# New engine orders for a fused linear-attention and squared-ReLU feed-forward kernel

## The chip, the cores and the metric

The kernel runs on one core of a Trainium2 chip. The metric is the device time of one execution in microseconds; the lower it is, the better. Three runs of the kernel before gave 171.85, 172.10 and 172.58 us, with a median of 172.1. One further execution was profiled; all rows below come from it.

## The reference

The first stage is a gated linear attention, a recurrence over 768 positions with a 48 x 48 state for each of 4 x 8 heads. The second is a feed-forward layer with a squared ReLU.

```python
# q, k, v, alpha: (4, 8, 768, 48), float32
for t in range(S):
    state = alpha[:, :, t, :, None] * state + np.einsum('bhd,bhe->bhde', k[:, :, t], v[:, :, t])
    y[:, :, t] = np.einsum('bhd,bhde->bhe', q[:, :, t], state)
x = y.transpose(0, 2, 1, 3).reshape(3072, 384)
h = x @ w_in                 # (384, 2048)
r = np.maximum(h, 0.0)
out = (r * r) @ w_out        # (2048, 384)
```

## The kernel before

**Units.** The 3072 tokens are cut into 12 units of 256 (four batches, three stretches of each). A unit's number stands in every name of the order: `p0_4` is the score step of unit 4.

**Attention of a unit g.** Four loads bring alpha, k, q and v (`lda`, `ldk`, `ldq`, `ldv`, lines 521 to 540) into one of four raw buffers. `pr` multiplies pairs of alpha, `ln` takes the logarithm, a matmul with a triangular matrix (`m1`, later `m1i` and `m1s`) makes running sums in PSUM, and `ei`, `ea`, `ec`, `es` take exponentials on ScalarE (`lm` and `lb` make the second set from unit 4 on; `bk` and `aq` multiply by alpha). `ekm` and `eqm` multiply k and q by them on VectorE. The results are transposed: for units 0 to 2 on TensorE (`tr`, with the copies `et` out of PSUM), from unit 3 on by two DMA transposes (`tr0_g`, `tr1_g`, line 745) that SyncE issues. `p0` makes the scores of all heads in two PSUM tensors, `mk0` and `mk1` (line 934) apply the causal mask on VectorE, `vc` casts v to bf16, `kv` makes the state's products (from unit 3 on inside the step `y` of the unit before), `sa`, `sc` and `sd` update the state, and `y` (lines 801 to 870) makes the attention's output in PSUM. `xe` copies it out, `xt` transposes it, on TensorE with the copy `xv` for units 0 to 6 and by a DMA transpose for units 7 to 11 (the tuple `DMA_X`, line 369).

**Feed-forward of a unit.** `s1_g_u` for u = 0 to 7 are the first layer's groups, six matmuls of 256 columns each; `re` is the ReLU of one group and `sq` the square of one or two (lines 1035 and 1045 to 1049). The second layer is plain for units 0, 1, 2 and 11 (`s2_g_j_s`: token half j, quarter s of the hidden width, four matmuls of 384 columns; `oe` copies the result out). For units 3 to 10 it is one level of Strassen's scheme (lines 1061 to 1142): seven products `m1` to `m7` in two halves each (`s2_g_m10` is the first half of m1; four matmuls of 192 columns), sums of the weights made once (`ws`), sums of the activations (`ga`, `gb`, `gc`, a half each, lines 1077 to 1080), and copies and additions `ca` to `cg` that collect the products in the output tile. `out` is the store of a unit.

**The order.** The dictionary `ORDERS` (lines 12 to 77) writes out for each of the five engines the list of names that it executes, one after the other; it also says which engine does a step that could be done by several (`RING`, line 79). Steps without a name have a number: `#0` to `#23` are the constants' fills. `Program.place` finds which earlier steps of other engines each step has to wait for, and `Program.emit` writes for each engine its list with these waits. An engine waits at the head of its list, so what stands behind a waiting step waits too. `lda` to `ldv`, `win`, `wout`, `tr`, `xt` and `out` are DMAs: in the list of SyncE (`sp`) or GpSimd (`pool`) stands their issue. `fill512` and `fill256` are matmuls on zeros in the list of TensorE (`pe`); nothing reads what they write. Some loads have a gate besides (the table `AFTER`): `lda2`, `ldk2`, `ldq2` and `ldv2` go out after `win1` has landed, `wout0` after `win2`, `wout1` after `ldk2`, the loads of unit 3 after `wout0`, `ldq1` and `win1` after `ldk0`.

**PSUM.** Eight banks of 2 KB: two `psX` and two `psZ` for the attention (`psZ` holds also the state products and, from unit 5 on, the running sums), `psWH` with one bank for the second layer (`W`) and two for the first (`H`), and `psO` for the second layer. `s2_2_1_0` writes `psO` after `oe2_0` has read it. Output tiles are two, used in turn: `oe2_0` writes the tile that `out0_1` stores.

Of the kernel before, what the change touches and what calls it, by code (L numbers as in the profile page):

```python
# [18 lines left out]
        ec7 re4_5 sq4_3 re4_6 es7 sq4_6 re4_7 re5_0 sq4_5 re5_1 lm8 re5_2 re5_3 ln8 xe6 ei8 ea8 re5_5 re5_4 es8 cc4
        re5_7 sq5_1 re5_6 lm9 sq5_3 sq5_6 re6_1 re6_0 xe7 ln9 re6_2 ei9 ea9 re6_4 re6_5 ca5 sq6_5 re6_6 es9 cc5 re6_7  # L20
        sq6_3 re7_0 lm10 re7_1 vc10 re7_2 ln10 xe8 ei10 ea10 re7_4 re7_5 sq7_3 re7_7 sq7_1 re7_6 re8_1 sq7_5 cc6 es10
        xe9 re8_2 sq7_6 ln11 sq7_7 lm11 ei11 ea11 es11 re8_5 ca7 re8_6 sq8_5 re8_7 sq8_1 re9_0 vc11 sq8_3 re9_1 re9_2
        xe10 re9_3 re9_5 re9_4 sq9_1 re9_7 re10_1 cc8 re10_3 re10_4 re10_5 sq10_1 re10_6 cc9 sq10_5 re11_1 sq10_7
# [11 lines left out]
        gc6_1 sa10 cd6 ce6 re8_4 ga7_1 re8_3 cg6 cf6 lb11 eqm1_11 gb7_1 eqm0_11 mk1_10 cb7 ekm11 cc7 mk0_10 sq8_7 cd7
        ce7 ga8_0 gb8_0 ga8_1 cg7 sa11 gb8_1 gc8_0 sq9_3 gc8_1 ca8 cf7 re9_6 mk1_11 sq9_7 re10_0 cb8 mk0_11 ga9_0
        re10_2 cd8 ce8 xe11 gb9_0 gb9_1 cf8 cg8 ca9 re10_7 sq10_6 cb9 re11_0 cd9 ce9 ga10_1 cg9 re11_2 gb10_1 gb10_0
        cf9 gc10_1 cc10 cb10 re11_4 cd10 ce10 sq11_5 cg10 re11_6 cf10 oe11_0 oe11_11
# [1222 lines left out]
```

## Time and profile before

| | us |
|---|---|
| median of three runs | 172.1 |
| lowest and highest | 171.85, 172.58 |
| profiled execution, its own time | 172.4 |
| span of the profiled execution | 170.7 |
| HBM read and written | 25.17 MB, 4.72 MB |

The span runs from the first to the last instruction of the profile; the execution's own time has 1.7 us more around it. A row of a timeline reads: start, duration, engine, line, operation, output tile from input tiles, form and count, and in brackets how long the engine stood idle just before and which event ended that wait. A row of a group has the busy time and the mean in ns of one instruction behind the bar. PE is TensorE (PEld its weight loads), DVE VectorE, ACT ScalarE, POOL GpSimd and SPq the queue of SyncE. Matmuls are pipelined: the duration of one includes its drain, and the pace is read from start to start. The releaser of a wait is inferred from semaphores: where the engine named had long been done it was another, often a DMA.

### The profile page before, as it was taken

Reading aid. Unit: us, or ns where it says so; the run is one execution under the profiler, and the core shown is the slowest. Engines: PE = TensorE matmul, PEld = TensorE weight load, DVE = VectorE, ACT = ScalarE, POOL = GpSimd, SP = SyncE. Lnnn points to the kernel's source line nnn. Section 1 sums busy time; section 2 is a strip of 40 time slices with the busy share of each in tenths; the row PEclk is TensorE's granted clock in tenths of the full one; section 3 lists DMA queues with packets and bytes.
Section 4 is the critical chain, followed back from the end, with each engine's and each line's share of the span. In section 5 each row is a group of like instructions: output and inputs, shape, how many; then the busy total and the mean of one; then the engine's idle time right before and its main releaser. Section 6 shows DMA issues by size and latency. Waiting matters only on the chain.

```text
span 170.7 us, 5620 instructions
## 1 busy us (share of the span) xinstructions
PE 162.1 (95%) x2428; PEld 140.2 (82%) x2428; DVE 137.0 (80%) x243; ACT 120.6 (71%) x213; POOL 89.1 (52%) x85
## 2 busy tenths in 40 slices
PE   6899999799999969999999999989999999999994
...
DMA  5999999998999999999999789999864920400222
GB/s 135 338 272 252 289 280 197 245 336 213 160 252 158 284 296 140 318 206 289 199 202 313 150 145 267 189 235 282 116 149 79 183 96 4 119 23 0 92 96 94
DMA packets 68233, 32.81 MB, mean 192 GB/s; under 512 B 64144, under 2 KB 65168, under 8 KB 68208
## 3 DMA queue, kind: packets, MB, share of 16 engines
...
HBM read 25.17 MB, written 4.72 MB: 175 GB/s over the span
## 4 chain that ended last, share of the span: by engine, by line
PE 60%; DMA 19%; DVE 10%; POOL 5%; SPq 2%; issue 1%; ACT 1%; DVEq 0%
PE psWH L1027 22%; PE psO L1093 11%; PE psWH L1093 9%; DMA raw<-in_k_dram 7%; DMA wout<-in_moe_w_out_dram 5%; PE psO L1165 5%; DMA win<-in_moe_w_in_dram 4%; DMA raw<-in_v_dram 3%; DVE pm L934 3%; DVE qks L734 3%; PE psX L826 2%; PE psZ L794 2%; PE psX L815 2%; PE psX L995 2%; PE psX L923 2%
## 5 line engine op out<-in xcount | busy, mean ns | idle before, releaser
L1027 PE MATMUL psWH<-xt,win 128*128 128x256 bf16 x552 | 72.1, 273 | 0.1
L1027 PEld LDWEIGHTS psWH<-xt,win 128*128 128x128 bf16 x552 | 59.8, 129 | 1.5 <-DVE xt L981 0.3
L1035 ACT ACTIVATE rr<-psWH 128x512 bf16<-128x512 f32 x73 | 42.4, 595 | 20.7 <-PE psWH L1027 19.9
L1049 ACT ACTIVATE gt<-rr 128x1024 bf16<-128x1024 bf16 (+1 forms) x37 | 33.9, 928 | 1.2 <-DVE rr L1037 1.1
L1048 POOL TENSOR_TENSOR gt<-rr 128x512 bf16<-128x512 bf16 (+1 forms) x11 | 16.3, 1479 | 19.6 <-ACT rr L1035 19.6
L1165 PE MATMUL psO<-wout,gt 128*128 128x384 bf16 x96 | 18.4, 326 | 1.2 <-DMA wout<-in_moe_w_out_dram 1.2
L934 DVE TENSOR_TENSOR pm<-psZ,caus 128x1024 bf16<-128x1024 f32 x12 | 14.6, 1219 | 2.4 <-PE psZ L923 2.4
L934 DVE TENSOR_TENSOR pm<-psX,caus 128x1024 bf16<-128x1024 f32 x12 | 14.6, 1216 | 1.4 <-PE psZ L923 1.1
L1080 POOL TENSOR_TENSOR sh<-gt 128x512 bf16<-128x512 bf16 x10 | 13.1, 1314 | 5.0 <-DVE gt L1079 3.7
L1093 PE MATMUL psWH<-sw,gt 128*128 128x192 bf16 x128 | 15.5, 246 | 0.0
L1037 DVE TENSOR_SCALAR rr<-psWH 128x512 bf16<-128x512 f32 x19 | 13.0, 686 | 3.0 <-PE psWH L1027 3.0
L1093 PE MATMUL psO<-wout,gt 128*128 128x192 bf16 x128 | 14.0, 246 | 0.0
L1165 PEld LDWEIGHTS psO<-wout,gt 128*128 128x128 bf16 x96 | 8.7, 97 | 6.2 <-DMA wout<-in_moe_w_out_dram 1.5
L734 DVE TENSOR_TENSOR qks<-raw,ek 128x768 bf16<-128x768 f32 x11 | 11.6, 1052 | 2.3 <-DMA raw<-in_k_dram 1.6
L1079 POOL TENSOR_TENSOR gt<-sg,gt 128x512 bf16<-128x512 bf16 x7 | 9.8, 1404 | 6.2 <-DVE sg L1077 6.1
L683 POOL TENSOR_TENSOR ek<-ek,raw 128x384 f32<-128x384 f32 x9 | 9.0, 1005 | 6.6 <-ACT ek L676 6.6
L1077 POOL TENSOR_TENSOR sg<-gt 128x1024 bf16<-128x1024 bf16 x3 | 6.4, 2132 | 9.7 <-PE psO L1093 8.3
L1093 PEld LDWEIGHTS psWH<-sw,gt 128*128 128x128 bf16 x128 | 10.9, 98 | 0.5
L729 DVE TENSOR_TENSOR qks<-raw,eq 128x384 bf16<-128x384 f32 x18 | 10.8, 612 | 0.3 <-ACT eq L702 0.2
L1077 DVE TENSOR_TENSOR sg<-gt 128x1024 bf16<-128x1024 bf16 x13 | 10.7, 824 | 0.3 <-PE psO L1093 0.2
L1093 PEld LDWEIGHTS psO<-wout,gt 128*128 128x128 bf16 x128 | 10.6, 98 | 0.4
L1124 DVE TENSOR_TENSOR osb<-psWH,osb 128x192 f32<-128x192 f32 x24 | 8.4, 352 | 2.4 <-PE psWH L1093 2.4
...
## 6 DMA issues: line engine op xcount, KB each, us to landing
raw<-in_q_dram SPq DMA_DIRECT2D x11, 384.0 KB, 5.8
out_dram<-osb SPq DMA_DIRECT2D x11, 384.0 KB, 4.2
raw<-in_alpha_dram SPq DMA_DIRECT2D x10, 384.0 KB, 4.5
raw<-in_k_dram SPq DMA_DIRECT2D x9, 384.0 KB, 5.2
raw<-in_v_dram SPq DMA_DIRECT2D x9, 384.0 KB, 4.9
...
raw<-in_k_dram POOLq DMA_DIRECT2D x3, 384.0 KB, 6.3
raw<-in_v_dram POOLq DMA_DIRECT2D x3, 384.0 KB, 7.6
```

The costliest lines, as they stand in the source:

```text
L729: add("dve", lambda e, j=j, dst=dst: e.tensor_tensor(dst, RAW[r][:, 2, :, j, :].rearrange("p (n x) d -> p n x d", x=2), EQ[la][:, j].rearr ...
L734: add("dve", lambda e, a=a, E=E: e.tensor_tensor(QKS[qs][:, a, :, :, 0:D], RAW[r][:, 1 + a].rearrange("p h j d -> p j h d"), E[la][:].rear ...
L934: add("dve", lambda e, hf=hf, psT=psT: e.tensor_tensor(PM[pm][:, hf].rearrange("p r n j t -> p (r n) (j t)"), psT[:, :, :].rearrange("p r ...
L1027: ins = pe.matmul(psF[:, i * T:(i + 1) * T], WIN[:, kk, hidden(fj)], mov, start=(kk == 0), stop=(kk == KT - 1))
L1035: add("act", lambda e, psF=psF, rr=rr: e.activation(rr, psF, AF.Relu), act_ns(512), pu + 600, reads=[keyF], writes=[("rr", rb, half)], nam ...
L1037: alts={"dve": (lambda e, psF=psF, rr=rr: e.tensor_scalar(rr, psF, 0.0, None, ALU.max), dve_ns(512))})
L1048: alts={"pool": (lambda e, dst=dst, sq=sq: e.tensor_tensor(dst, sq, sq, ALU.mult), 200 + k * 840), "act": (lambda e, dst=dst, sq=sq: e.act ...
L1049: "act": (lambda e, dst=dst, sq=sq: e.activation(dst, sq, AF.Square), act_ns(k * 512))})
L1077: ga = lambda e, us=us: e.tensor_tensor(SG[:, us], view(us, 128, [[0, 2], [1, 128]]), view(us, 0, [[384, 2], [1, 128]]), ALU.subtract)
L1080: gc = lambda e, us=us: e.tensor_tensor(SH[:, us], G4[:, us, 1, 0], G4[:, us, 0, 1], ALU.add)
L1093: ins = pe.matmul(psS, left(u), right(u), start=(first and u == 0), stop=(u == nu - 1), skip_group_check=True)
L1165: ins = pe.matmul(psS, GT[gt][:, fj, j, :], WOUT[:, fj, :], start=(fj == 0), stop=(fj == FT - 1))
```

## The change

Only the text of `ORDERS` is changed. Its diff is cut to what is spoken of later; the other lines of the five lists are likewise rewritten.

```diff
     "act": """
-        table ln0_0 ln1_0 ei0_0 ea0_0 ei1_0 ec0_0 et00_0 ea1_0 ec1_0 #23 et01_0 et11_0 ln1 ei1 ea1 xe0 ec1 et0_1 re0_1
-        vc1 re0_0 sq0_1 re0_3 xe1 re0_4 ln2 re0_6 ei2 re0_7 es2 vc2 re0_5 ea2 re1_1 re1_3 sq0_6 et0_2 ec2 sq0_7 sq1_3
...
+        table #23 ln0_0 ln1_0 ei0_0 ea0_0 ei1_0 ea1_0 et00_0 ec1_0 ec0_0 vc0 et11_0 ln1 ei1 ea1 xe0 xv0 ec1 vc1 re0_0
+        re0_1 re0_2 re0_3 sq0_1 re0_4 ln2 re0_7 ei2 sq0_3 re0_5 es2 ea2 sq0_5 re1_3 re1_4 re1_5 ec2 re1_6 et1_2 re1_7
...
     "dve": """
-        et1_2 re1_4 ws0_0 ws2_0 re1_6 mk1_2 pr3 sq1_7 ws0_1 sa2 mk0_2 ekm3 sc2 eqm1_3 aq3 eqm0_3 pr4 oe1_0 xv2 sa3 sc3
-        lb4 ekm4 eqm1_4 eqm0_4 mk0_3 mk1_3 re2_5 oe1_1 xe3 sa4 xv3 sq2_7 sc4 lb5 eqm1_5 ekm5 mk1_4 mk0_4 eqm0_5 ws1_0
...
-        mk1_8 ga6_0 cd5 sq6_7 sa9 ce5 re7_3 gc5_0 lb10 cf5 ga6_1 ekm10 cg5 mk1_9 ca6 mk0_9 cb6 re8_0 eqm1_10 eqm0_10
...
+        eqm2 et0_2 #4 ws0_0 ws2_0 ws3_0 mk1_2 pr3 ws0_1 sa2 sc2 mk0_2 ekm3 eqm1_3 aq3 pr4 eqm0_3 oe1_0 sa3 xv2 ws2_1
+        sc3 lb4 eqm1_4 eqm0_4 ekm4 mk1_3 mk0_3 re2_5 ws1_0 xe3 sa4 sc4 sq2_7 xv3 bk5 eqm1_5 lb5 ekm5 mk1_4 mk0_4
+        eqm0_5 oe2_0 sa5 sc5 ga3_0 ws1_1 xv4 re3_7 lb6 eqm1_6 eqm0_6 ekm6 mk1_5 mk0_5 ca3 ga3_1 re4_2 sa6 sc6 gc3_0
...
+        eqm1_9 eqm0_9 mk0_8 mk1_8 cd5 re7_1 re7_2 ce5 sa9 re7_3 ga6_1 gb6_0 re7_5 cf5 cg5 lb10 ekm10 mk1_9 mk0_9
...
+        ekm11 mk1_10 gc7_0 sq8_7 cd7 sd7 ga8_0 ce7 ga8_1 sa11 cg7 gb8_0 cf7 sq9_3 mk0_11 cb8 mk1_11 cc8 cd8 re10_1
+        ga9_1 ga9_0 ce8 cf8 re10_5 cg8 re10_6 gc9_0 ca9 cb9 cc9 cd9 ce9 re10_7 cg9 re11_2 ca10 ga10_1 cf9 re11_3 cb10
...
     "pe": """
-        fill256_8 tr01_0 fill256_9 p0_0 tr11_0 kv0 fill256_10 p1_0 fill256_11 fill256_12 m11 y0 fill512_13 fill512_14
-        fill512_15 fill256_16 tr0_1 xt0 tr1_1 fill256_17 s1_0_1 p0_1 s1_0_0 s1_0_2 kv1 s1_0_3 y1 s1_0_4 s1_0_6 xt1
-        s1_0_7 m1i2 m1s2 s1_1_2 s1_1_0 s1_1_1 s1_0_5 s1_1_3 s1_1_5 tr0_2 s1_1_4 tr1_2 s1_1_6 s2_0_0_0 p0_2 s2_0_0_1
-        s1_1_7 s2_0_0_2 s2_0_0_3 s2_0_1_0 kv2 m1i3 s2_0_1_1 s2_1_0_0 s2_0_1_2 s2_1_0_1 m1s3 s2_1_0_2 y2 s2_1_0_3
-        s2_0_1_3 xt2 m1i4 s2_1_1_0 s1_2_0 s1_2_1 s2_1_1_1 s1_2_2 s1_2_3 p0_3 s1_2_4 s1_2_5 s2_1_1_2 s2_1_1_3 y3 s1_2_6
-        s1_2_7 xt3 m1i5 s2_2_0_0 s1_3_0 s1_3_1 p0_4 s2_2_0_1 s1_3_2 s1_3_3 s2_2_0_2 s2_2_0_3 y4 s1_3_5 s1_3_4 m1i6
-        s2_2_1_0 s1_3_7 s2_2_1_1 xt4 s2_2_1_2 s2_2_1_3 s1_3_6 p0_5 s1_4_1 s1_4_0 s2_3_m10 s2_3_m11 s2_3_m60 s1_4_2
...
-        s2_5_m40 s1_7_3 s2_5_m41 m1i10 s1_7_4 s1_7_5 s2_5_m30 s2_5_m31 s1_7_6 s1_7_7 p0_9 s2_6_m60 s2_6_m10 s2_6_m11
...
+        fill512_8 fill256_9 fill256_10 tr01_0 p0_0 tr11_0 kv0 fill256_11 p1_0 fill256_12 fill256_13 m11 fill256_14 y0
+        fill512_15 fill512_16 fill512_17 tr0_1 xt0 tr1_1 fill512_18 fill512_19 fill512_20 fill256_21 p0_1 s1_0_0
+        s1_0_2 s1_0_1 kv1 s1_0_3 y1 s1_0_4 s1_0_6 s1_0_7 xt1 m1i2 m1s2 s1_0_5 s1_1_1 s1_1_2 s1_1_0 tr0_2 s1_1_4 s1_1_3
+        s1_1_5 s1_1_6 s1_1_7 tr1_2 s2_0_0_0 s2_0_0_1 p0_2 s2_0_1_0 s2_0_0_2 s2_0_0_3 kv2 m1i3 s2_0_1_1 s2_1_0_0
+        s2_1_0_1 s2_1_0_2 m1s3 s2_0_1_2 y2 s2_1_0_3 s2_0_1_3 xt2 m1i4 s2_1_1_0 s1_2_0 s1_2_1 s2_1_1_1 s1_2_2 s1_2_3
+        p0_3 s2_1_1_2 s1_2_5 s1_2_4 s2_1_1_3 y3 s2_2_0_0 s1_2_7 s1_2_6 xt3 m1i5 s2_2_0_1 s2_2_0_2 s1_3_0 s1_3_1 p0_4
+        s1_3_2 s1_3_3 s2_2_0_3 s1_3_4 y4 s2_2_1_0 s1_3_5 m1i6 xt4 s2_2_1_1 s1_3_7 s2_2_1_2 s2_2_1_3 s1_3_6 s1_4_1 p0_5
...
+        s2_5_m71 s1_7_1 s2_5_m50 s1_7_2 y8 s2_5_m51 s1_7_3 s2_5_m40 s1_7_4 s2_5_m41 s2_5_m30 m1i10 s1_7_5 s2_5_m31
+        s1_7_6 s1_7_7 s2_6_m10 s2_6_m11 p0_9 s2_6_m20 s2_6_m60 s1_8_0 s1_8_1 s2_6_m21 s1_8_2 y9 s2_6_m61 s2_6_m50
...
+        s2_8_m11 s2_8_m61 s1_10_1 s1_10_0 s2_8_m20 s2_8_m21 s2_8_m70 y11 s2_8_m71 s1_10_2 s2_8_m50 s2_8_m51 s1_10_3
+        s2_8_m40 s1_10_4 s2_8_m41 s1_10_5 s2_8_m30 s2_8_m31 s1_10_6 s2_9_m10 s2_9_m60 s2_9_m61 s2_9_m11 s1_11_0
...
     "pool": """
-        #22 #15 #14 #21 #20 lda1 ldk1 win0 vc0 win1 ldv1 win2 lda2 ldq2 ldk2 ldv2 wout0 wout1 aq2 sq1_1 ldk3 ldv3
-        ws3_0 bk3 pr6 sd2 bk4 vc4 pr5 ws2_1 sd3 bk5 vc5 sd4 gb3_0 bk6 sq3_6 vc6 gb3_1 gc3_1 sd5 bk7 sq4_7 vc7 pr8
...
-        gb7_0 bk11 gc7_1 sq8_6 sd7 gc7_0 sq9_5 sq9_6 ga9_1 gc9_0 gc9_1 sq10_3 ga10_0 gc10_0 sq11_7
+        #15 #21 #22 #20 #14 lda1 win0 ldk1 ldq1 win1 ldv1 win2 lda2 ldk2 ldq2 ldv2 wout0 sd1 wout1 vc2 aq2 sq0_7 sq1_3
+        ldk3 ldv3 sq1_7 bk3 pr6 sd2 bk4 vc4 sd3 pr5 sq2_5 vc5 sd4 sq3_3 gb3_0 bk6 sq3_6 vc6 pr7 gb3_1 sd5 bk7 sq4_7
...
+        sd6 pr11 gc6_1 gb7_0 gb7_1 vc11 bk11 gc7_1 gb8_1 sq9_7 sq9_5 gc8_1 gc8_0 gb9_0 gb9_1 gc9_1 sq10_6 ga10_0
+        sq10_7 gb10_0 gb10_1 gc10_0 sq11_3 sq11_5 sq11_7
     """,
     "sp": """
-        lda0 ldk0 ldq0 ldv0 ldq1 lda3 ldq3 lda4 lda6 ldq4 ldk4 tr1_3 tr0_3 ldv4 lda5 ldq5 tr1_4 tr0_4 ldk5 ldv5 out0_1
-        ldq6 ldk6 out1_1 tr0_5 tr1_5 ldv6 lda7 ldq7 ldk7 out2_1 tr1_6 tr0_6 ldv7 lda8 ldk8 ldv8 tr1_7 tr0_7 ldq8 lda9
-        ldk9 ldv9 ldq9 out3_1 tr0_8 tr1_8 xt7 lda10 ldv10 ldk10 tr1_9 lda11 tr0_9 xt8 out4_1 ldq10 ldq11 ldk11 out5_1
...
+        lda0 ldk0 ldq0 ldv0 lda3 ldq3 lda4 lda6 ldq4 ldk4 tr0_3 tr1_3 ldv4 lda5 ldk5 ldq5 tr0_4 tr1_4 ldv5 out0_1 ldk6
+        ldq6 out1_1 tr0_5 tr1_5 ldv6 lda7 ldq7 ldk7 tr0_6 tr1_6 ldv7 lda8 ldk8 out2_1 tr0_7 tr1_7 ldq8 ldv8 lda9 ldv9
+        ldk9 ldq9 out3_1 tr0_8 tr1_8 xt7 lda10 ldv10 ldk10 tr0_9 out4_1 tr1_9 xt8 ldq10 lda11 ldv11 out5_1 ldq11
...
```

Counted over the whole text, 160 names stand on another engine than before: 28 go from ScalarE to VectorE and 27 back, 19 from VectorE to GpSimd and 12 back, 9 from ScalarE to GpSimd and 7 back, and one load (`ldq1`) moves from SyncE's list to GpSimd's. TensorE's list has 14 fills of 512 columns and 8 of 256, before 10 and 8. Nothing outside `ORDERS` is touched.

68 lines of the change are left out of this document (32 added, 36 removed).

## The prediction

> **What bounds the kernel now.** I read the page's busy shares and slices first, then the busy time by stage, then TensorE's own timeline for the places where it stands still, and last the chain of waits and the SyncE, VectorE and GpSimd timelines around each of those places.
>
> ```profile
> PE 162.1 (95%) x2428; PEld 140.2 (82%) x2428; DVE 137.0 (80%) x243; ACT 120.6 (71%) x213; POOL 89.1 (52%) x85
> PE   6899999799999969999999999989999999999994
> DMA  5999999998999999999999789999864920400222
> ```
>
> TensorE is the bound, with two dents in the middle (slices 8 and 15, near 32 and 62 us). The DMA engines are full until 85 us, so loads have a floor of their own there. By stage:
>
> ```profile
> 16.00:36.00 20.00, 18.43 (x263) 15.47 (x264) 16.56 (x27) 14.71 (x25) 11.37 (x11) 1.00 1.06 260
> 36.00:62.00 26.00, 24.48 (x384) 18.50 (x384) 21.43 (x35) 19.79 (x39) 10.59 (x11) 1.00 1.02 231
> 62.00:74.00 12.00, 12.00 (x234) 10.46 (x226) 10.73 (x19) 11.30 (x22) 5.08 (x5) 1.00 1.23 254
> ...
> 110.00:122.00 12.00, 11.29 (x189) 10.69 (x188) 9.75 (x18) 9.53 (x17) 6.84 (x6) 1.00 0.99 228
> ```
>
> The first column after the length is TensorE's busy time, and the granted clock is 1.00 throughout. Up to 62 us it misses 1.6 and 1.5 us; from 62 to 74 nothing, and the slices read nine until 110; from there 0.7. So an order can win little but the stalls, and they have names:
>
> ```profile
> 34.36 1.48 PE L1165 MATMUL psO<-wout,gt 128*128 128x384 bf16 x8 [1.23 <-DMA wout<-in_moe_w_out_dram]
> 48.01 0.42 PE L923 MATMUL psX<-kqt 64*64 64x128 bf16 x16 [0.24 <-DVE qks L729]
> 61.63 0.19 PE L815 MATMUL psX<-sbd,kqt 64*128 64x48 bf16 x1 [1.28 <-DVE pm L934]
> 113.06 0.42 PE L923 MATMUL psX<-kqt 64*64 64x128 bf16 x16 [0.71 <-DVE osb L1124]
> ```
>
> In the order's names these are `s2_0_0_2` (second half of w_out), `p0_3`, `y4` and `p0_9`; together 3.46 us.
>
> **The change part by part.** No instruction of the computation changes. 160 names change engine, nearly all names change place, and TensorE gets four more 512-column fills. That units 4 to 6 transpose x on TensorE is in the kernel before already (`DMA_X` starts at 7, and the row below counts six transposes for each of units 0 to 6), so this costs and saves nothing.
>
> ```profile
> L969 PE MATMUL psX<-ident,xbf 128*128 128x128 bf16 x42 | 3.5, 219 | 0.0
> 13.36 0.93 PE L1228 MATMUL psO<-zero 128*128 128x512 bf16 x4
> 15.94 0.68 DVE L764 COPY kqt<-psZ 128x1024 bf16<-128x1024 bf16 x1
> ```
>
> *Fills and opening.* Four fills are about 0.9 us (the row holds three of 512 and one of 256). Four of the new list (three of 512, one of 256) stand between `tr1_1` and `p0_1`, which waits for `et1_1` until 16.6 anyway (the copy's row), so they fill a wait. Then `p0_1` comes before any group of `s1_0`, and TensorE goes into 17 us about 0.4 us behind. Ahead of the wait for w_out, `s2_0_1_0` (four matmuls, 0.65 us in the chain's steps) is now put before `s2_0_0_2`. So TensorE reaches w_out's second half with 0.65 more done, and up to all 1.23 us of that stall can go. But the next stop is `p0_3`:
>
> ```profile
> 38.91 0.96 DVE L734 TENSOR_TENSOR qks<-raw,ek 128x768 bf16<-128x768 f32 x1 [0.25 <-POOL ek L683]
> 39.78 0.55 DVE L896 TENSOR_TENSOR tmp<-psZ,smd 128x384 f32<-128x384 f32 x1
> 41.89 3.35 SPq L745 DMA_TRANSPOSE kqt<-qks  x2
> kqt<-qks SPq DMA_TRANSPOSE x18, 4.7
> ```
>
> `p0_3` reads the transposed keys and queries of unit 3. The two transposes are issued at 41.89, as soon as `eqm0_3` is done, the second about 1.7 us later (43.6); with the median landing of 4.7 us that is 48.3, where `p0_3` in fact starts at 48.01. VectorE's `eqm0_4`, which the wait row names, is nothing that `p0_3` reads, so I take the transposes for the cause. In the new VectorE order `sc2` (0.55) leaves the stretch from `ekm3` to `eqm0_3` and `pr4` enters it, of the same length (0.555 in its group); the start of that stretch hangs on unit 3's alpha, whose load waits for w_out's first half. So this floor stays at 48.0, and I count the opening at **0**. Its bounds: 1.23 us gained if the floor moves up as well, 1.7 lost if unit 3's loads come late (first rival).
>
> `ldq1` moves from SyncE, where it went out at 5.43, to GpSimd's queue behind `lda1`, `win0` and `ldk1`, about 7.1 by my count of three issues from 4.4 on, some 0.9 each (`ldv3`'s row further down). The one q load of that queue took 7.1 to land: so it lands near 14.2, when `eqm1` begins at 14.23. If it is 0.8 late, that is covered by the same floor.
>
> ```profile
> 5.43 0.37 SPq L537 DMA_DIRECT2D raw<-in_q_dram  x1
> 14.23 0.95 DVE L734 TENSOR_TENSOR qks<-raw,eq 128x768 bf16<-128x768 f32 x1
> raw<-in_q_dram POOLq DMA_DIRECT2D x1, 384.0 KB, 7.1
> ```
>
> *The stall at 61.63.* The chain of waits goes from the transposes of unit 4 to unit 5's k, to `ekm5`, to the two mask products of unit 4 behind it on VectorE, to `y4`:
>
> ```profile
> 48.57 4.93 SPq L745 DMA_TRANSPOSE kqt<-qks  x2
> 53.54 1.36 SPq L537 DMA_DIRECT2D raw<-in_k_dram  x1
> 55.60 1.11 SPq L1181 DMA_DIRECT2D out_dram<-osb  x1
> 56.34 0.42 PE L923 MATMUL psX<-kqt 64*64 64x128 bf16 x16
> 58.35 0.96 DVE L734 TENSOR_TENSOR qks<-raw,ek 128x768 bf16<-128x768 f32 x1 [1.60 <-DMA raw<-in_k_dram]
> 59.31 2.28 DVE pm L934 x2
> 62.68 1.53 PE L1027 MATMUL psWH<-xt,win 128*128 128x256 bf16 x12
> 61.89 0.49 ACT L1172 ACTIVATE osb<-psO 128x384 f32<-128x384 f32 x1 [1.99 <-DMA out_dram<-osb]
> ```
>
> `ldk5` now stands ahead of `ldq5` and of both transposes, so k lands before 54 instead of 58.26, and `ekm5` (behind `bk5`, which VectorE now does in 0.56) can run by 57.5. The transposes go out 1.4 us later (one load's issue); `p0_4` has two more groups of `s2_2` before it (1.3 us) as cover. After `p0_4` (near 57.65) two mask products need 2.3, and TensorE has four groups, 2.6 us, to do. The 1.28 us go. Part comes back at once: behind `y4` stands `s2_2_1_0`, which writes the bank that `oe2_0` empties; `oe2_0` (now on VectorE, 0.555) waits for the store `out0_1`, whose issue has the same steps ahead of it as before and so its 55.60, and which landed at 61.89. So `s2_2_1_0` starts about 62.5, when `y4` (some 1.0 long, 61.63 to 62.65) would have ended at 61.9 with `s1_3_4` done. Before, the group behind `y4` began at 62.68, so `y4` ended near 62.65, without `s1_3_4` (0.66, half of that row's two groups from start to start). Gain 62.65 - 62.5 + 0.66 = **0.81** (ends 0 and 1.28).
>
> *The stall at 113.06.* `s2_6_m10` and `m11` (0.33 each, four matmuls) now come before `p0_9` instead of behind it, and `cg5`, which frees their bank, no longer queues behind `ga6_1` and `ekm10`. Whatever `p0_9` waits for, the second transpose of unit 9 by my reading (106.83 plus 4.7 to 6.1), they fill 0.66 of 0.71. Between unit 9's transposes `out4_1` takes the place of `lda11`, 0.58 each:
>
> ```profile
> 106.21 0.58 SPq L537 DMA_DIRECT2D raw<-in_alpha_dram  x1
> 106.83 2.48 SPq L745 DMA_TRANSPOSE kqt<-qks  x1
> 110.68 0.58 SPq L1142 DMA_DIRECT2D out_dram<-osb  x1
> ```
>
> Gain **0.66** (ends 0 and 0.71).
>
> *Moved work.* Priced by the groups' means, the moves give GpSimd 14.4 us more, and take 3.7 from VectorE and 1.5 from ScalarE, so loads become 103, 133 and 119 us under TensorE's 162: none becomes the bound by its sum. By place a move can hurt, above all a half-sum of the second layer, of which GpSimd makes three times the time:
>
> ```profile
> L1079 POOL TENSOR_TENSOR gt<-sg,gt 128x512 bf16<-128x512 bf16 x7 | 9.8, 1404 | 6.2 <-DVE sg L1077 6.1
> L1079 DVE TENSOR_TENSOR gt<-sg,gt 128x512 bf16<-128x512 bf16 x9 | 4.1, 476 | 0.0
> L1077 DVE TENSOR_TENSOR sg<-gt 128x1024 bf16<-128x1024 bf16 x13 | 10.7, 824 | 0.3 <-PE psO L1093 0.2
> 127.62 1.53 DVE L734 TENSOR_TENSOR qks<-raw,ek 128x768 bf16<-128x768 f32 x1
> 128.30 1.87 POOL L1080 TENSOR_TENSOR sh<-gt 128x512 bf16<-128x512 bf16 x1
> ```
>
> New stalls that I can't place: nothing at the low end, at the high end 1.28, the largest that this kernel has; I take 0.2, about its smallest, since every stall that I could trace got ready work put in front of it.
>
> **Sum** against the profiled execution: 172.4 - 0.81 - 0.66 + 0.2 = 171.1 (span 169.4). The runs' median lies 0.3 under that execution, so 170.8.
>
> **The rivals.** *The opening gives it back.* GpSimd now issues `ldk3` and `ldv3` behind `vc2`, `aq2`, `sq0_7` and `sq1_3`; before, behind `aq2` and `sq1_1`, `ldv3` at 31.80. For it: ScalarE now squares `sq0_3` and `sq0_5` ahead of `re1_3`, which `sq1_3` reads. If that makes the loads 2.7 us late, v of unit 3 lands near 41.5 (34.5 and some 7 of the 7.6 that is the median there), its cast on ScalarE ends at 42.3, and `y2`, now at 40.64, is 1.7 late, and the floor with it: 172.1 - 1.47 + 1.7 = 172.3. Against it: my count of ScalarE's new order gives only 0.5 us.
>
> ```profile
> 31.80 0.89 POOL L537 DMA_DIRECT2D raw<-in_v_dram  x1
> raw<-in_v_dram POOLq DMA_DIRECT2D x3, 384.0 KB, 7.6
> 40.64 0.36 PE L855 MATMUL psX<-smd,kqt 128*64 128x96 bf16 x8
> ```
>
> *Slower: the half-sums.* In units 7, 9 and 10 both `gb` halves run one after the other on GpSimd. From `s2_8_m51` to `s2_9_m61` TensorE has 4.6 us of other groups; the path through `ga9_1`, `ga9_0` (0.82 each) and `gb9_0`, `gb9_1` (1.40 each) is 4.44. One collision with VectorE stretched `ekm10` from 0.96 to 1.53 and the sum beside it from 1.16 to 1.87. From the first collision in a unit on, it is late by about 0.5, with two by 1.1; and 1.1 in each of units 9 and 10, with 0.9 for the squares of unit 11 that queue behind them, is 3.1 (unit 7 has 0.9 us of slack by the same count): 172.1 - 1.47 + 3.1 = 173.7. By the Trainium skill ("SBUF — State Buffer", Who interferes with whom) VectorE and GpSimd hold a shared port as an exclusive lock for a whole instruction, so a collision would cost up to a full GpSimd operation, 1.4; with two in each of two units that is near 5 us, about 176. Rows agree that they collide, at 0.6 to 0.7.
>
> *More than forecast.* The loads' floor moves up too (w_out's first half earlier, as `win1` and `win2` no longer queue on GpSimd behind the cast `vc0`) and the 1.23 go as well: 169.6. Against it: full DMA engines.
>
> **Chances.** Forecast 0.40 (its own range 170.1 to 171.6), opening gives back 0.22, half-sums 0.26, more than forecast 0.12. No change means within 0.5%, 0.86 us, about what the runs can tell. Faster: 0.36 of the forecast's and the 0.12, 0.48. Same: 0.04 of the forecast's, 0.18 of the opening's, 0.03 of the half-sums', 0.25. Slower: the other 0.27. The range reaches to 169.4 for the last rival and to 173.9 for the half-sums.
>
> **What would show it.** Right: no idle of TensorE before `y4`, k of unit 5 landed by 54, a wait of some 0.6 at `s2_2_1_0` on `oe2_0`, none at `p0_9`, `p0_3` still near 48.0. Wrong: `p0_3` before 47 or after 49, or waits of TensorE on GpSimd's `gb` lines in units 9 and 10, or a stall over 1 us in a place not named here.

## The result and the profile after

| | before | changed |
|---|---|---|
| median of the first comparison, 4 runs each | 172.18 us | 173.41 us |
| lowest and highest | 171.85, 172.58 | 173.17, 173.47 |
| profiled execution, own time and span | 172.4, 170.7 | 173.35, 171.6 |

The ratio is 1.0068, 95% interval 1.0044 to 1.0091: 0.7% slower, where 170.8 us, 0.8% faster, was forecast. The time lies inside the range, on the other side of no change. As the experiments will show, this number has a partner: in three later sets, of 12 runs each, the same changed kernel came out at 0.995, 0.9967 and 0.9964 of the kernel before. The ratios here and below leave out runs over 1.5% above the fastest of their kernel (the profiled ones of e9 and e16 are such), so they can differ a little from the quotients of the medians. The traces show where an execution loses time; how often one does is not settled. The reading starts with the slower result.

From the page of the changed kernel: the busy shares, and TensorE's busy tenths in 40 slices.

```profile
PE 163.6 (95%) x2432; PEld 141.1 (82%) x2432; DVE 137.5 (80%) x237; ACT 119.8 (70%) x210; POOL 101.0 (59%) x95
PE   6899999999989999999999799999999999999994
```

The two old dents (slices 8 and 15) are gone; a new one is at slice 23, near 97 us, and a slight one at slice 12, near 49 us. By stage, in the windows view of the same execution (length, busy time of PE, PEld, DVE, ACT, POOL, then clock, DMA share and GB/s):

```profile
74.00:86.00 12.00, 11.64 (x201) 10.72 (x200) 11.22 (x22) 9.82 (x19) 7.51 (x7) 1.00 1.16 183
86.00:98.00 12.00, 11.31 (x187) 10.35 (x184) 10.68 (x16) 9.51 (x17) 9.34 (x8) 1.00 1.12 272
98.00:110.00 12.00, 11.45 (x189) 10.89 (x190) 10.52 (x20) 9.57 (x18) 6.66 (x6) 1.00 1.00 203
110.00:122.00 12.00, 12.00 (x197) 11.40 (x195) 10.63 (x17) 10.29 (x19) 9.56 (x8) 1.00 1.05 222
```

From 110 us on the 0.71 that TensorE missed before is filled. But between 74 and 110, where it read nine tenths in every slice before, it now misses 0.36, 0.69 and 0.55: 1.60 us. TensorE's timeline of the changed kernel names the places (and, for the sum below, the starts of `y5` and `y8`):

```profile
48.37 0.42 PE L925 MATMUL psX<-kqt 64*64 64x128 bf16 x16 [0.68 <-DVE qks L736]
58.40 0.42 PE L925 MATMUL psX<-kqt 64*64 64x128 bf16 x16 [0.39 <-issue]
62.08 0.18 PE L817 MATMUL psX<-sbd,kqt 64*128 64x48 bf16 x1 [0.30 <-POOL vbf L726]
72.69 0.19 PE L817 MATMUL psX<-sbd,kqt 64*128 64x48 bf16 x1
85.65 0.18 PE L817 MATMUL psX<-sbd,kqt 64*128 64x48 bf16 x1 [0.36 <-issue]
94.83 0.19 PE L817 MATMUL psX<-sbd,kqt 64*128 64x48 bf16 x1 [0.44 <-DVE pm L936]
98.55 0.32 PE L667 MATMUL psZ<-lab,linc 128*128 128x384 bf16 x1 [0.78 <-ACT rr L1037]
108.03 0.19 PE L817 MATMUL psX<-sbd,kqt 64*128 64x48 bf16 x1
```

In names: `p0_3`, `p0_4`, `y4`, then a wait inside `y6`, one ahead of `y7` and one ahead of `m1i9`. The lines are those of before plus 2. The stretch from `y2` to `y5` took 32.14 us, before 31.99, with 0.32 more work in it: 0.17 won. From `y5` to `y8` it took 35.34, before 33.75 (72.63 to 106.38), with one group of 0.66 less in it: 2.25 lost. The wait rows there show 1.58 of that, as the drain of the matmul ahead of a wait counts as busy. From `y8` to the end it took 63.59, before 64.29, with a half product of 0.33 more in it: 1.03 won, 0.74 of it at `p0_9` (start to start against the pace of the groups). The span ends 0.9 later.

The two waits at 94.83 and 98.55 are one chain. The timeline of SyncE's queue, VectorE and GpSimd in the same execution:

```profile
80.85 5.54 SPq L747 DMA_TRANSPOSE kqt<-qks  x2
86.44 0.58 SPq L539 DMA_DIRECT2D raw<-in_q_dram  x1
91.04 1.20 DVE L731 TENSOR_TENSOR qks<-raw,eq 128x384 bf16<-128x384 f32 x1 [0.50 <-DMA raw<-in_q_dram]
92.44 1.21 DVE L936 TENSOR_TENSOR pm<-psZ,caus 128x1024 bf16<-128x1024 f32 x1
93.57 1.21 DVE L936 TENSOR_TENSOR pm<-psX,caus 128x1024 bf16<-128x1024 f32 x1
95.19 2.20 POOL L1050 TENSOR_TENSOR gt<-rr 128x1024 bf16<-128x1024 bf16 x1
96.22 1.72 DVE L1079 TENSOR_TENSOR sg<-gt 128x1024 bf16<-128x1024 bf16 x1
97.86 0.55 DVE L891 TENSOR_TENSOR smd<-psZ,sbd 128x384 bf16<-128x384 f32 x1
```

The pair of transposes of unit 7 holds SyncE's queue for 5.54 us; `ldq8` goes out behind it at 86.44; `eqm0_8` waits 0.50 for q, and itself takes 1.20, where it takes 0.55 in executions without the wait; the masks of unit 7 stand behind `eqm0_8` in VectorE's list and end at 94.78, when `y7` starts. That is the first wait. Then `ga5_0` starts at 96.22, a microsecond into the GpSimd square `sq5_5` (95.19 to 97.39), and takes 1.72; alone it takes 0.68. `sa8`, which empties the bank that `m1i9` writes, stands behind it and ends at 98.41, and `m1i9` starts at 98.55. (The wait row names a ReLU of ScalarE, as releasers are inferred; by the code it is `sa8`.) That is the second wait.

### The profile page after: what moved, and what is told of

It reads as the page before. It is cut to its first block, busy times and chain, and to the rows that moved or that the text cites. A ratio compares the mean times of both kernels' runs of the same rounds, so it can differ in the third digit from the quotient of the medians.

```text
span 171.6 us, 5617 instructions
## 1 busy us (share of the span) xinstructions
PE 163.6 (95%) x2432; PEld 141.1 (82%) x2432; DVE 137.5 (80%) x237; ACT 119.8 (70%) x210; POOL 101.0 (59%) x95
## 4 chain that ended last, share of the span: by engine, by line
PE 57%; DMA 23%; DVE 7%; POOL 5%; SPq 3%; ACT 2%; issue 1%; DVEq 0%; ACTq 0%
PE psWH L1029 23%; PE psO L1095 11%; PE psWH L1095 8%; DMA win<-in_moe_w_in_dram 7%; DMA raw<-in_alpha_dram 5%; DMA wout<-in_moe_w_out_dram 5%; PE psO L1167 4%; DVE pm L936 3%; SPq L747 3%; DMA raw<-in_v_dram 3%; DMA raw<-in_q_dram 3%; POOL raw L539 2%; PE psX L828 2%; PE psX L997 2%; PE psX L925 1%; PE psX L817 1%
## 5 line engine op out<-in xcount | busy, mean ns | idle before, releaser
L1037 ACT ACTIVATE rr<-psWH 128x512 bf16<-128x512 f32 x70 | 41.1, 594 | 20.7 <-PE psWH L1029 19.8
L1050 POOL TENSOR_TENSOR gt<-rr 128x512 bf16<-128x512 bf16 (+1 forms) x18 | 26.4, 1472 | 11.4 <-ACT rr L1037 11.4
L1081 POOL TENSOR_TENSOR gt<-sg,gt 128x512 bf16<-128x512 bf16 x11 | 13.0, 1183 | 13.7 <-DVE sg L1079 13.7
L1039 DVE TENSOR_SCALAR rr<-psWH 128x512 bf16<-128x512 f32 x22 | 15.0, 683 | 1.9 <-PE psWH L1029 1.8
L1082 POOL TENSOR_TENSOR sh<-gt 128x512 bf16<-128x512 bf16 x11 | 13.6, 1249 | 1.6 <-DVE gt L1081 1.4
L731 DVE TENSOR_TENSOR qks<-raw,eq 128x384 bf16<-128x384 f32 x18 | 13.0, 733 | 0.8 <-DMA raw<-in_q_dram 0.5
L726 POOL CAST vbf<-raw 128x768 bf16<-128x768 f32 x7 | 6.5, 928 | 11.6 <-DMA raw<-in_v_dram 11.2
L1167 PEld LDWEIGHTS psO<-wout,gt 128*128 128x128 bf16 x96 | 8.8, 98 | 4.8
L956 ACT ACTIVATE xbf<-psX 128x768 bf16<-128x768 f32 x10 | 8.1, 810 | 5.9 <-PE psX L817 5.0
L736 DVE TENSOR_TENSOR qks<-raw,ek 128x768 bf16<-128x768 f32 x11 | 10.7, 973 | 1.8 <-ACT ek L643 1.0
```

Source lines behind the costliest of these rows:

```text
L731: add("dve", lambda e, j=j, dst=dst: e.tensor_tensor(dst, RAW[r][:, 2, :, j, :].rearrange("p (n x) d -> p n x d", x=2), EQ[la][:, j].rearr ...
L736: add("dve", lambda e, a=a, E=E: e.tensor_tensor(QKS[qs][:, a, :, :, 0:D], RAW[r][:, 1 + a].rearrange("p h j d -> p j h d"), E[la][:].rear ...
L1037: add("act", lambda e, psF=psF, rr=rr: e.activation(rr, psF, AF.Relu), act_ns(512), pu + 600, reads=[keyF], writes=[("rr", rb, half)], nam ...
L1039: alts={"dve": (lambda e, psF=psF, rr=rr: e.tensor_scalar(rr, psF, 0.0, None, ALU.max), dve_ns(512))})
L1050: alts={"pool": (lambda e, dst=dst, sq=sq: e.tensor_tensor(dst, sq, sq, ALU.mult), 200 + k * 840), "act": (lambda e, dst=dst, sq=sq: e.act ...
L1081: gb = lambda e, us=us: e.tensor_tensor(G4[:, us, 0, 1], SG[:, us, 1], G4[:, us, 0, 0], ALU.subtract)
```

## The experiments

Two theories stood against each other. **Theory Q**: the loss comes from when SyncE's queue gets a load out, which differs from execution to execution. **Theory C**: it is built into the order of the compute engines. Ratios are to the kernel before in the same set of runs. Each set ran on a chip of its own. The diffs show only the stretch of a list that changes.

### First set: one edit for each stall

`e1_q8_early`: the load ahead of the store and of the transposes.

```diff
-ldk8 out2_1 tr0_7 tr1_7 ldq8 ldv8
+ldk8 ldq8 out2_1 tr0_7 tr1_7 ldv8
```

> The changed kernel with one load moved in SyncE's list: ldq8 ahead of out2_1 and of unit 7's two transposes. Theory (lost in the queue): q of unit 8 landed at 90.95, VectorE stood 0.50 us for it ahead of both mask products of unit 7, and y7 stood 0.44 us. With q8 out at about 79.3 it lands near 85, eqm0_8 runs at 90.5 at once, the wait at y7 goes, and the kernel is about 0.5 us faster than the changed kernel: near 172.9. Rival (the load is only the last of several): eqm0_8 still collides with GpSimd's square, or the transposes of unit 7, now one issue later, hold p0_7 (90.0) instead, and the time stays at 173.4 within 0.2.

`e2_sa8_first`, on VectorE:

```diff
-ga5_0 sa8
+sa8 ga5_0
```

> The changed kernel with two neighbours on VectorE exchanged: sa8 ahead of ga5_0. Theory (port collision behind which the state's sum queues): ga5_0 took 1.72 us beside GpSimd's square sq5_5 (95.19 to 97.39) instead of 0.69, sa8 came out at 98.41, and m1i9, which overwrites what sa8 reads, stood 0.78 us. With sa8 first, m1i9 starts near 97.7 and the kernel is 0.7 to 0.9 us faster than the changed kernel: near 172.6. Rival (m1i9 waits for ln9 or re6_3, as the wait row with its ScalarE releaser has it): no change, 173.4 within 0.2.

`e3_v5_pool`: v of unit 5 is issued by GpSimd (and `EITHER` names unit 5 as one whose v may be).

```diff
-tr0_4 tr1_4 ldv5 out0_1      # sp
-bk4 vc4                      # pool
+tr0_4 tr1_4 out0_1
+bk4 ldv5 vc4
```

> The changed kernel with ldv5 issued by GpSimd behind bk4 (about 46.2) instead of by SyncE behind unit 4's transposes (55.49). Theory (the stall at y4 moved from k5 to v5): v5 lands near 53, vc5 ends long before y4, y4 starts when s1_3_4 is done, near 61.6 instead of 62.08, and 0.3 to 0.5 us are won: near 173.0. Rival (the loads' queue paces unit 5 in any case): another wait of the same length at y4 or at s2_2_1_0 on oe2_0, whose store now goes out one issue earlier; 173.4 within 0.2.

`e4_three`: all three edits.

> The changed kernel with all three moves: ldq8 ahead of unit 7's transposes, sa8 ahead of ga5_0, ldv5 on GpSimd. Theory: the waits at y4, y7 and m1i9 are separate losses on TensorE's path and add: 0.4 + 0.5 + 0.8 = 1.7, so 171.7, 0.3% under the kernel before. Rival: what is won at y4 and y7 is waited for at the next floor, and only the last one, at m1i9, counts: 172.6.

Measured beside 31 runs of the kernel before (median 171.92, 170.41 to 174.06), 10 runs each:

| | median us | ratio and interval |
|---|---|---|
| e1_q8_early | 171.08 | 0.9955 (0.9915 to 0.9995) |
| e2_sa8_first | 171.16 | 0.9968 (0.9933 to 1.0003) |
| e3_v5_pool | 172.9 | 1.002 (0.9967 to 1.0072) |
| e4_three | 173.25 | 1.0083 (1.0039 to 1.0128) |

Three edits that were each to take a stall away don't add up, and single runs of one kernel now lie 3.6 us apart. The changed kernel itself was not in this set; e1 and e2 come out where it does in the later ones, so neither edit is shown to gain anything in the median. In e4's profile the third edit did harm at a place of its own: v of unit 4 and v of unit 5 now go out together (45.45 on SyncE, 45.95 on GpSimd), the cast `vc4` of the first ends at 52.90 (51.55 in the first profile), and `y3` waits 1.67 for it, in e3 0.17. The telling line is in a trace: in e3, whose order behind 62 us is that of the changed kernel word for word, TensorE waits neither at `y6` nor at `y7` nor at `m1i9`. A fixed price for each place, with which these four were planned, was wrong: the stalls come and go with the execution.

In e1 the transposes were as slow as in the first profile, and the load stood ahead of them:

```profile
78.81 1.15 SPq L539 DMA_DIRECT2D raw<-in_q_dram  x1
...
81.20 5.16 SPq L747 DMA_TRANSPOSE kqt<-qks  x2
```

and TensorE has no wait between 84 and 101 us: in this execution the length of the pair costs nothing, with `ldq8` ahead of it.

### Second set: the changed kernel again, and the lists exchanged

`e5_changed_again` has no edit.

> The changed kernel, unchanged, beside three kernels of the same job. Theory Q (the loss comes from when SyncE's list issues loads and transposes, and so from one run's timing): 1 us above the kernel before, 172.9 where that is 171.9, but in its trace the three stalls of the first profile (0.5 us inside y6, 0.6 at y7, 0.9 at m1i9) come back at other places or with other sizes, and not all three. Theory C (the loss is built into the order of the compute engines): the same 1 us, with the same three stalls again within 0.2 us each.

171.72 us (169.69 to 174.25, 12 runs; before 172.35 in 21 runs): ratio 0.995 (0.9904 to 0.9996). In this set the change comes out 0.5% faster, and in the profile all three stalls of units 6 to 8 are absent. Theory C is gone as it stood; theory Q, too, had expected a loss of 1 us, at other places.

`e6_before_new_sp` and `e7_changed_old_sp` exchange SyncE's whole list (in e6 `ldq1` goes to GpSimd behind `ldk1`).

```diff
# e6, in the kernel before
-"sp": (list of before)
+"sp": (list of the changed kernel)
# e7, in the changed kernel
-"sp": (list of the changed kernel)
+"sp": (list of before, without ldq1)
```

> The kernel before with SyncE's list of the changed one (ldq1 on GpSimd behind ldk1, as there). Theory Q: slower than before by about 1 us (172.9 where before is 171.9), the first stalls behind y4, at masks of units 6 to 8 that wait for q. Theory C: within 0.4 us of the kernel before.

> The changed kernel with SyncE's list of the kernel before (ldq1 stays on GpSimd). Theory Q: about 1 us faster than the changed kernel of this job, 171.9 where that is 172.9, though the stall at y4 goes back to about 1.3 us with ldk5 behind the transposes. Theory C: as the changed kernel, or slower by the 0.2 us that y4 had gained.

176.69 and 176.95 us in 6 runs each: 1.0247 (1.0188 to 1.0306) and 1.0266 (1.0207 to 1.0325). Neither theory had that: each list of SyncE is fitted to its own compute lists, and the wrong one costs 4 us, whichever of the two it is. In e6 TensorE loses much of it early: `y2` starts at 43.39, before 40.64. Two rows of that stretch are the wait for the second half of w_out (1.23 before) and that of the running sums of unit 3 for the logarithm of its alpha, which before has no wait:

```profile
35.44 1.48 PE L1165 MATMUL psO<-wout,gt 128*128 128x384 bf16 x8 [1.58 <-DMA wout<-in_moe_w_out_dram]
39.61 0.34 PE L665 MATMUL psWH<-lab,linc 128*128 128x384 bf16 x1 [1.60 <-ACT lab L656]
```

So the exchange doesn't isolate SyncE's share.

`e8_before_m10`: one term of the forecast alone, in the kernel before.

```diff
-s1_7_7 p0_9 s2_6_m60 s2_6_m10 s2_6_m11
+s1_7_7 s2_6_m10 s2_6_m11 p0_9 s2_6_m60
```

> The kernel before with one edit of the change: s2_6_m10 and s2_6_m11 ahead of p0_9 on TensorE. By the prediction's second term the wait of 0.66 us ahead of p0_9 goes and the time falls by 0.66 (171.2 where before is 171.9). Rival: the masks of unit 9 come 0.7 us later with p0_9 and the wait turns up at y9, time as before.

173.59 us, 1.0052 (1.0002 to 1.0102): no gain. Rows of its timeline:

```profile
81.31 4.35 SPq L745 DMA_TRANSPOSE kqt<-qks  x2
85.71 1.36 SPq L537 DMA_DIRECT2D raw<-in_q_dram  x1
90.93 1.14 DVE L729 TENSOR_TENSOR qks<-raw,eq 128x384 bf16<-128x384 f32 x1 [1.13 <-DMA raw<-in_q_dram]
94.39 0.19 PE L815 MATMUL psX<-sbd,kqt 64*128 64x48 bf16 x1 [0.53 <-DVE pm L934]
...
114.10 0.83 PE L1093 MATMUL psO<-wout,gt 128*128 128x192 bf16 x8 [0.43 <-DVE osb L1124]
```

Two things are to be seen. The wait ahead of `p0_9` is gone, but `s2_6_m10` itself waits 0.43, for the copy that empties its bank: two groups moved without VectorE's list bring almost nothing (from `y8` to the end 64.20, before 64.29). And the chain at `y7` is in the order of before as well: the pair took 4.35 instead of 3.48, `eqm0_8` waited 1.13 for q, `y7` 0.53, and the stretch from `y5` to `y8` took 35.13 instead of 33.75.

### Third set: the chain at unit 8, and the other term alone

`e9_changed_third` has no edit.

> The changed kernel a third time, unchanged, beside three edits of it and of the kernel before. If the sign of the first comparison belongs to the order (theory C), the ratio is above 1 again, about 1.007, and the masks of unit 7 or the running sums of unit 9 stall TensorE in its trace. If it belongs to how long SyncE's pair of transposes of unit 7 takes (theory Q: 5.54 us where it was slower, 4.28 us where it was faster), the stalls at y7 and m1i9 come back where that pair takes over 5 us, and are absent under 4.5 us.

`e10_q8_and_sa8` has the edits of e1 and e2.

> The changed kernel with ldq8 ahead of out2_1 and the transposes of unit 7 on SyncE, and sa8 ahead of ga5_0 on VectorE. Theory Q: q8 has landed before 88 us whatever the transposes take, no stall at y7 and none at m1i9, 0.5 to 1.5 us below the changed kernel of this job where that one has the stalls, equal to it where not. Theory C: the same time as the changed kernel of this job within 0.4 us, since the stalls only turn up at another step.

`e12_q8_late`:

```diff
-ldq8 ldv8 lda9 ldv9 ldk9
+ldv8 lda9 ldv9 ldq8 ldk9
```

> The changed kernel with ldq8 three places later on SyncE, behind ldv8, lda9 and ldv9 (0.58, 1.86 and 1.16 us in the first profile, 3.6 us in all): the suspected cost doubled. Theory Q: y7 waits for the masks behind eqm0_8 for some 2 to 3.5 us, and the time is 2 to 3 us above the changed kernel of this job. Theory C: VectorE's list absorbs it, under 1 us.

| | median us (before 172.83, 29 runs) | ratio and interval |
|---|---|---|
| e9_changed_third, 12 runs | 172.37 | 0.9967 (0.9921 to 1.0014) |
| e10_q8_and_sa8, 12 runs | 172.61 | 0.9963 (0.9916 to 1.0009) |
| e12_q8_late, 6 runs | 176.39 | 1.021 (1.0162 to 1.0257) |

In e9's profile the pair took 4.79, between the two bounds that theory Q had named, and both waits are back (0.46 ahead of `y7`; `ga5_0` takes 1.72 again, and `m1i9` comes 1.0 late by its start). In e10 neither is there, and its profiled execution took 170.49 against 172.94 for e9; yet the medians agree, where theory Q had 0.5 to 1.5 between them. So the chain's effect on an execution is plain, and its share in the median is not measured by this pair. e12 shows what the place can cost:

```profile
87.77 1.21 SPq L539 DMA_DIRECT2D raw<-in_q_dram  x1
...
92.89 0.56 DVE L731 TENSOR_TENSOR qks<-raw,eq 128x384 bf16<-128x384 f32 x1 [3.33 <-DMA raw<-in_q_dram]
...
93.78 0.83 PE L1095 MATMUL psWH<-sw,sg 128*128 128x192 bf16 x8 [1.05 <-DVE osb L1126]
96.04 0.19 PE L817 MATMUL psX<-sbd,kqt 64*128 64x48 bf16 x1 [1.43 <-DVE pm L936]
```

The load goes out 3.14 us later than in e5 (84.63), VectorE stands 3.33 us and TensorE loses 1.05 and 1.43: `y5` to `y8` takes 35.92, against 33.05 in e5. The median rises by 4.0 against e9, more than the 2 to 3 expected. Not all of that is `ldq8`: in e12's profile another 1.56 is lost at `y10`, at 135.06, behind the k load of unit 11 (see the fourth set).

`e11_before_k5`: the first term of the forecast alone, in the kernel before.

```diff
-lda5 ldq5 tr1_4 tr0_4 ldk5 ldv5
+lda5 ldk5 ldq5 tr1_4 tr0_4 ldv5
```

> The kernel before with one edit of the change: ldk5 ahead of ldq5 and of the transposes of unit 4. By the first term of the prediction y4 starts 1.28 us earlier and 0.81 us stay: 0.81 us below the kernel before. Rival: ldv5, still behind the transposes, takes the place of ldk5, y4 starts 0 to 0.3 us earlier, and the time is as before.

172.66 us, 0.9998 (0.9968 to 1.0028): nothing. The rows of its timeline that answer to those of the forecast:

```profile
49.55 4.78 SPq L745 DMA_TRANSPOSE kqt<-qks  x2
56.99 0.42 PE L923 MATMUL psX<-kqt 64*64 64x128 bf16 x16 [0.55 <-issue]
60.93 0.19 PE L815 MATMUL psX<-sbd,kqt 64*128 64x48 bf16 x1
62.86 1.21 PE L1027 MATMUL psWH<-xt,win 128*128 128x256 bf16 x9 [0.33 <-issue]
```

The 1.28 at `y4` are gone, and `y4` starts 0.70 earlier (61.63 before). But the transposes went out 0.98 later (48.57), `p0_4` starts 0.65 later (56.34) with a wait of 0.55, and a group behind `y4` waits 0.33. At `y5`, 72.48 against 72.63, 0.15 is left. It was not v that took k's place, as my rival had it: here v was in time.

### Fourth set: controls and the two other parts

`e13_changed_fourth` and `e14_before_again` have no edit.

> The changed kernel a fourth time. Theory Q: its profile has the stalls at y7 and m1i9 if eqm0_8 waits for q8, and neither if it does not; ga5_0 takes 1.7 us where it starts after the GpSimd square sq5_5 has begun and under 0.8 us where it starts before. The ratio to the kernel before is between 0.99 and 1.01, with no sign of its own. Theory C: above 1.004 and both stalls.

> The kernel before, unchanged, for a second profile. Theory Q: its waits move too, by half a microsecond or more at y4 (1.28 in the first profile) or elsewhere between 40 and 100 us, while the wait ahead of p0_9 (0.66), which no load ends, comes back within 0.2 us. Theory C: all of them come back within 0.2 us.

`e15_halfsums_dve`: `gb9_0`, `gb9_1`, `gb10_0`, `gb10_1` leave GpSimd's list.

```diff
# dve
-ce8 cf8
+ce8 gb9_0 gb9_1 cf8
-ga10_1 cf9
+ga10_1 gb10_1 gb10_0 cf9
```

> The changed kernel with gb9_0, gb9_1, gb10_0 and gb10_1 back on VectorE. By the prediction's rival on the half-sums 1 to 3 us faster than the changed kernel of this job. By the first profile, in which TensorE waits at no line of them: the same within 0.4 us.

`e16_fewer_fills`:

```diff
-fill512_15 fill512_16 fill512_17 tr0_1 xt0 tr1_1 fill512_18 fill512_19 fill512_20
+fill512_17 tr0_1 xt0 tr1_1 fill512_20
```

> The changed kernel without four of its fills of 512 columns (0.85 us of TensorE between 13 and 17 us). By the prediction's floor at p0_3 the stall there grows by as much and the time stays within 0.3 us of the changed kernel of this job. Rival: 0.8 us faster, since the opening bounds the rest.

| | median us of 12 runs (before 171.63, 35 runs) | ratio and interval |
|---|---|---|
| e13_changed_fourth | 171.21 | 0.9964 (0.9925 to 1.0003) |
| e14_before_again | 172.75 | 1.0059 (1.0018 to 1.01) |
| e15_halfsums_dve | 172.53 | 1.0045 (1.0003 to 1.0087) |
| e16_fewer_fills | 171.11 | 0.9944 (0.9903 to 0.9985) |

(One run of e13, 323.18 us, and one of before, 232.61, stand far outside.) e14 is the kernel before measured against itself: 0.6% apart, with an interval that leaves 1 out. The intervals take the runs for independent draws, and they are not; a difference under about 0.6% of one set decides nothing here. That holds for the 1.0068 of the first comparison, nearly, and for each 0.996 alone; three of them on three chips are worth more, though not shown to be enough.

The profile of e14 fits neither expectation. No wait of TensorE between 40 and 100 us moved by half a microsecond (`y4` 1.10, before 1.28), and the one at `p0_9`, which was to come back within 0.2, is 1.02 where it was 0.71. On VectorE one did move:

```profile
90.79 0.56 DVE L729 TENSOR_TENSOR qks<-raw,eq 128x384 bf16<-128x384 f32 x1 [0.81 <-ACT rr L1035]
```

The row names a ReLU, but q, issued at 84.72, landed at 90.70, 0.09 ahead of this start, the same step as in the other waits for q (0.09 to 0.10): `eqm0_8` stood 0.81 for q, and TensorE lost nothing by it. What differs is GpSimd's square `sq5_7`, which also started at 90.79: here `eqm0_8` took its usual 0.56 and the square 1.46. In the first profile, e7, e8, e9 and e16 `eqm0_8` started 0.10 to 0.39 behind the start of that square and took 1.07 to 1.35, the square 1.04. So in these profiles a late q cost TensorE time only where it put `eqm0_8` behind the start of that square, or, in e12, where `eqm0_8` waited 3.33.

e15 is not faster than the changed kernel of its set. In the first profile TensorE waits at no line of the half-sums, so there was nothing to free; with them on VectorE a group of unit 11 waits 0.56 for its ReLU, at 160.47.

In e16 `p0_3` starts at 47.84 with a wait of 0.47, in e13 at 47.81 with 0.52: the four fills come out and the time stays (171.11 against 171.21). The wait did not grow by 0.85 as expected; the gained time was used up before `y2`, which starts at 40.23 against 40.16.

In e13 the pair was short, and the same rows as in the first profile read:

```profile
79.88 3.24 SPq L747 DMA_TRANSPOSE kqt<-qks  x2
83.16 1.23 SPq L539 DMA_DIRECT2D raw<-in_q_dram  x1
88.95 0.55 DVE L731 TENSOR_TENSOR qks<-raw,eq 128x384 bf16<-128x384 f32 x1
93.56 0.78 DVE L1079 TENSOR_TENSOR sg<-gt 128x1024 bf16<-128x1024 bf16 x1
93.75 2.34 POOL L1050 TENSOR_TENSOR gt<-rr 128x1024 bf16<-128x1024 bf16 x1
94.26 0.55 DVE L891 TENSOR_TENSOR smd<-psZ,sbd 128x384 bf16<-128x384 f32 x1
```

With the pair 2.3 us shorter, `eqm0_8` doesn't wait, `ga5_0` starts 0.19 ahead of the square instead of 1.03 behind its start and takes 0.78 instead of 1.72, and TensorE doesn't wait once between 84 and 101 us.

e5 has no wait there either, but one further on, of the same kind:

```profile
123.78 0.58 SPq L539 DMA_DIRECT2D raw<-in_k_dram  x1
128.90 0.96 DVE L736 TENSOR_TENSOR qks<-raw,ek 128x768 bf16<-128x768 f32 x1 [1.49 <-DMA raw<-in_k_dram]
131.05 0.19 PE L817 MATMUL psX<-sbd,kqt 64*128 64x48 bf16 x1 [0.55 <-DVE pm L936]
```

These are `ldk11`, `ekm11` and `y10`; the mask `mk1_10` stands behind `ekm11`. This one belongs to the change. In the list of before `ldk11` stands ahead of unit 10's transposes and goes out at 113.08, 14.5 us before `ekm11`; in the new list it stands behind them and behind `xt9`, and went out at 122.16 to 125.53 in the six profiles of the table below with that list as it is. In five of them VectorE stood for it, 0.12 to 1.49, and in e5 TensorE lost 0.55.

### All profiles together

The stretch from the first matmul of `y5` to that of `y8` has the same groups in every kernel of one order. In the changed order it holds one first-layer group (0.66) less than before: `s1_4_3` stands ahead of `y5` there (and two half products, one at each end, have changed sides).

| execution | pair of unit 7, us | `ldq8` issued | `eqm0_8` waits for q | `y5` to `y8`, us | own time, us |
|---|---|---|---|---|---|
| before | 3.48 | 84.57 | no | 33.75 | 172.40 |
| e14_before_again | 3.52 | 84.72 | 0.81 | 33.75 | 172.84 |
| e11_before_k5 | 3.50 | 84.44 | no | 33.74 | 171.98 |
| e8_before_m10 | 4.35 | 85.71 | 1.13 | 35.13 | 173.62 |
| changed, first | 5.54 | 86.44 | 0.50 | 35.34 | 173.35 |
| e9_changed_third | 4.79 | 85.88 | 0.35 | 34.65 | 172.94 |
| e16_fewer_fills | 5.22 | 86.10 | 0.36 | 35.06 | 173.07 |
| e5_changed_again | 4.28 | 84.63 | no | 33.05 | 171.57 |
| e13_changed_fourth | 3.24 | 83.16 | no | 33.05 | 170.50 |
| e15_halfsums_dve | 3.06 | 84.25 | no | 33.05 | 172.67 |
| e1_q8_early | 5.16 | 78.81 | no | 33.05 | 171.22 |

Of the other profiles, e3 took 33.05 (`ldq8` at 84.06) and e12 35.92; those with `sa8` moved (e2, e4, e10) took 33.33 to 33.49 without a wait for q; with the lists of SyncE exchanged e6 took 33.74 and e7 34.60 (`ldq8` at 84.92, a wait of 0.64).

In the changed order of the table the stretch is 33.05 or it is 1.6 to 2.3 longer, in that of before 33.75 or 1.4 longer, and the long ones are those where `ldq8` went out after 85.7. The limit is not sharp: q was late in e7, issued at 84.92, and in time in e2, issued at 84.79, as it landed 5.3 and 4.0 after its issue. Both orders have the trap; without it the changed one does the stretch as fast as before (33.05 + 0.66 against 33.75).

## Why the prediction was wrong, step by step

- **Opening, counted 0: right.** The wait for w_out is gone in every profile of the changed order; `p0_3` starts at 48.37, in the repeats at 47.8 to 48.3, against 48.01. The floor of the transposes holds, as e16 shows from the other side.
- **Stall at `y4`, 0.81: mis-sized, 0.17 from `y2` to `y5`.** k was in time as forecast and the wait at `s2_2_1_0` didn't come. The step that failed is that the two groups put ahead of `p0_4` would cover the later transposes. In the changed kernel these went out 2.17 later (50.74), where 1.4 was reckoned with: besides k's load, now ahead as well, the q load took 2.20 instead of 1.23. `ldv5` behind them went out only at 55.49:

```profile
48.50 2.20 SPq L539 DMA_DIRECT2D raw<-in_q_dram  x1
50.74 4.71 SPq L747 DMA_TRANSPOSE kqt<-qks  x2
55.49 1.30 SPq L539 DMA_DIRECT2D raw<-in_v_dram  x1
...
61.11 0.82 POOL L726 CAST vbf<-raw 128x768 bf16<-128x768 f32 x1 [5.62 <-DMA raw<-in_v_dram]
```

  `p0_4` waited 0.39, `y4` 0.30 for v, `p0_3` 0.68 where it had waited 0.24: 1.13 of the 1.28 came up again at three places. e11 shows the same trade with this edit alone.
- **Wait at `p0_9`, 0.66: right in size, 0.71 of TensorE's time filled.** The size is in part luck: three profiles with the order of before at this place have 0.71, 1.02 (e14) and 0.43 (e11) there. The two groups alone don't do it: e8, with VectorE's list of before, moved the wait to `s2_6_m10`. VectorE's half alone was not run.
- **New stalls, 0.2: this is the step that failed most, and that turned the sign.** In the first profile they cost 2.29 between `y5` and `y8`, in e9 1.60 and in e16 2.01 (against the 33.05 of e5 and e13, which have none there). The wait inside `y6` is in the first profile only, and its cause was not found. "Every stall that I could trace got ready work put in front of it" was reasoned on one execution as if its times belonged to the order, and looked at the old stalls alone. `ldq8` stands behind the transposes of unit 7 in both lists and the pair starts at nearly the same time (80.85, before 81.04); only its length differed. The slack was never looked at: in the profile of before q landed at 89.59 and `eqm0_8` started at 89.79, so 0.20 us. Nor was the slack that the new list takes away, 14.5 us from the issue of `ldk11` to `ekm11` before and 5.1 in the first profile, where `ekm11` waited.
- **The rivals.** That GpSimd's late loads give the opening back: no, `y2` starts at 40.55 against 40.64. The half-sums: no, TensorE waits at no such line in units 9 and 10, and e15 with them on VectorE is not faster. Collisions of VectorE with GpSimd, which that rival priced, did cost time, but at `eqm0_8` and `ga5_0`. More than forecast: `p0_3` didn't move forward.
- **The moved work.** The page has 101.0, 137.5 and 119.8 us for GpSimd, VectorE and ScalarE, forecast 103, 133 and 119: VectorE did not get lighter. And counted from the two lists, 103 names change engine, the sum of the parts listed with the diff, not 160.

Put together, the two profiled executions of the unedited changed kernel that escape the chain at `y7` (e5, e13) ended 0.83 and 1.90 below the first profile of before; those that fall into it lose 1.6 to 2.3 there and, by the own times in the table, ended 0.5 to 1.0 above it. The medians of the three later sets lie 0.4 to 0.6 under those of before; that they are a mixture of the two kinds is likely and not shown, as the own times also differ by other stretches (e14 and e15 are near 172.8 without a loss at `y7`). The profiled run of the first comparison was of the second kind; that the three others, within 0.3 us of it, were too is inferred and not shown. Open stays why the pair takes 3.1 us one time and 5.5 another, and so whether the changed list (with the store `out2_1` just ahead of it, where before had `ldv8`) makes the long pair more frequent: the six profiles of the table with the changed list of SyncE as it is gave 3.06 to 5.54, the four with `ldv8` there 3.48 to 4.35, too few to tell. No version tried is faster than the changed kernel by more than two sets of one kernel differ.
